# BigBird attention followed by a GELU MLP on one core: dense first batch, one load queue in need order, a hand-set instruction order

## The chip, the cores and the metric

The kernel runs on one core of one Trainium2 chip. The metric is the device time of the core in microseconds (us). Most executions of one kernel agree within 0.5%. One execution of the kernel before fell into a slower state (341.37 us at a mean granted clock of 0.846) and is left out.

Engines are named as in the profile: PE is TensorE's matrix products, PEld its weight loads, DVE is VectorE, ACT is ScalarE, POOL is GpSimd, SP only starts DMAs. All instructions pass through one helper, so the profile gives them all the same source line (L54); groups are told apart by tile names.

## The reference, cut to what matters

```python
# q, k, v: (4 batches, 8 heads, 768 tokens, 64), float32; blocks of 32 tokens, 24 blocks
scores = q @ k.T / sqrt(64)
mask = |block_i - block_j| <= 1  or  block_i in (0, 23)  or  block_j in (0, 23)
mask |= three sampled key blocks for each query block
attn = softmax(where(mask, scores, -1e9))
x = (attn @ v).transpose(0, 2, 1, 3).reshape(3072, 512)
out = gelu(x @ w_in) @ w_out          # w_in (512, 2048), w_out (2048, 512), exact GELU
```

The work goes by half batches of 384 tokens: eight times attention, then a hidden layer (products with `w_in`, then GELU), then output products with `w_out`. They are counted 0 to 7 below; batch 0 is half batches 0 and 1.

## The kernel before

Attention exists in two forms. The *gathered* form (`scores`, `weighted`) computes only the blocks that the mask allows: POOL gathers the sampled key blocks (`gather_k`) and value blocks (`gather_v`) into their own tiles, which needs index arithmetic on DVE and a rotated copy of v in SBUF. The *dense* form (`first_scores`, `first_weighted`) computes all scores and adds the mask as a second product. Before, only the first half of batch 0 is dense.

These are the loads of the opening. The queue of SP takes the first keys and queries, the sampled indices and v; the queue of POOL takes the rest. The weights wait: a one-column memset ordered behind v's casts holds `w_in` back, and `w_out` follows it.

```python
for i, (w, x) in enumerate((("k", k), ("q", q))):
    ...                                           # two heads of k, then of q, as float32
    sp.dma_start(out=first_st[w], in_=x[0, 0:2].rearrange("h (p j) d -> p h (j d)", j=NT))
    if i == 0:
        sp.dma_start(out=raw, in_=...)            # the sampled indices
first_v = load_v(0, sp)                           # six DMAs, each row of 64 values is 256 bytes

def load_v(b, eng, after=None):
    t = stv_pool.tile([P, NT, H, D], F32, tag="st_v", name="st_v")
    ...
    for n in range(NT):
        eng.dma_start(out=t[:, n], in_=v[b, :, n * P:n * P + P].rearrange("h p d -> p h d"))

def after_values():
    for n in range(NT):
        own_v(0, first_v, n, n + 1, dve)          # float32 to bf16
    for c in range(2):
        dve.memset(w_in_sb[:, 0:1, 1024 * c:1024 * c + 1], 0.0)
        load_w_in(c)                              # casting DMA on POOL's queue
```

This is the order of the opening. Each engine runs its instructions in the order in which the program names them, so what stands in `extra` delays what follows on the same engine.

```python
extra = {(0, 3): lambda: first_pair(1), (1, 1): lambda: first_pair(2), (1, 3): lambda: first_pair(3),
         (2, 1): lambda: [after_values(), value_validity()],
         (2, 3): lambda: [first_weighted(0), gather_constants(), key_indices()],
         (3, 1): lambda: [first_weighted(1), load_w_out(0), load_w_out(1)]
         + [f() for f in k_steps(0, 1, range(NPAIR))],
         (3, 3): lambda: [first_weighted(2), rotate_first(), value_columns()]}
for hp in range(NPAIR):
    for t in range(NT):
        first_scores(hp, t)
        extra.get((hp, t), lambda: None)()
first_weighted(NPAIR - 1)
for m in range(MH):
    transpose_x(0, 0, m, st)
value_indices(0, dve)
```

After the opening, rules spread the work. `spread` strews the transposes and gathers for the next half evenly over the eight hidden steps, and `weave` puts a fixed number of output products behind each attention step. A hidden step takes all four 128-row parts of x at once:

```python
def step(m):
    hp_ = sc_pool.tile([P, 2, 512], F32, tag="sc", name="hp")
    for i in range(2):
        for ki in range(KIN):                     # KIN is 4
            pe.matmul(hp_[:, i, 0:HALF], lhsT=w_in_sb[:, ki, (m + i) * P:(m + i + 1) * P],
                             rhs=xT[:, ki, :], start=(ki == 0), stop=(ki == KIN - 1))
    act.activation(g[:, m:m + 2, :], hp_[:, :, 0:HALF], AF.Gelu)
```

The softmax here doesn't subtract the row's maximum and nothing guards it: scores larger than these inputs give would overflow.

## Time and profile before

| | kernel before |
|---|---|
| time, median of 3 runs | 321.12 us (319.97 to 321.38) |
| span of the profiled run, mean granted clock | 320.1 us, 0.973 |
| TensorE busy | 273.6 us, 85% of the span |
| first hidden product / second hidden layer starts | 37.6 us / 81.5 us |

From the page of the profile of before: the span; busy time by engine; busy tenths of PE and the granted clock in 40 slices of 8 us; then, of its list of DMA issues, the load of `w_out`, with its size and the time from issue to landing.

```profile
span 320.1 us, 8104 instructions
PE 273.6 (85%) x3560; PEld 163.4 (51%) x3560; DVE 136.8 (43%) x366; ACT 156.1 (49%) x206; POOL 100.7 (31%) x149
...
PE   1778596698993998989997998989997989899995
PEclk9999899799996899999999999999999999999999
...
w_out_sb<-in_moe_w_out_dram POOLq DMA_DIRECT2D x2, 1024.0 KB, 32.3
```

TensorE is the bottleneck, but the slices show holes in the opening (the first digits) and one near 96 to 104 us (the 3), with the clock reduced behind some of them. `w_out` took 32 us from its issue at 24.8 us.

The view of what each engine waited for names the holes of PE (total us, times, longest):

```profile
PE s L54 <- POOL kg L54: 5.7, 2, 5.1
PE op L54 <- DMA w_out_sb<-in_moe_w_out_dram: 5.1, 2, 3.1
...
PE psx L54 <- DVE x L54: 2.0, 1, 2.0
```

`s <- kg` is a score product that waits for gathered keys; `op <- w_out` an output product that waits for its weights; `psx <- x` the transposition of x that waits for its normalisation.

The timeline of before around the last of these (start, length, engine, operation, in brackets the idle time before it and who ended it):

```profile
34.06 0.85 DVE L54 SCALAR_TENSOR_TENSOR base_v<-colf,slotm,base_v 128x22 f32<-128x22 f32 x3
35.35 0.56 DVE L54 TENSOR_TENSOR x<-og,rc 128x384 bf16<-128x384 f32 x1
35.96 0.45 PE L54 MATMUL psx<-ident,x 128*128 128x128 bf16 x5 [2.00 <-DVE x L54]
37.60 4.42 PE L54 MATMUL hp<-xT,w_in_sb 128*128 128x384 bf16 x16 [0.52 <-DVE xT L54]
```

DVE does index arithmetic (from 31.35 us on, `base_v` is the end of it) for the gathers of the next half first, and only then normalises the last head pair, for which PE has long been waiting.

A view of chosen stretches. I cut the run where a hidden layer's first product starts, and once (51.4 us) where the first hidden layer ends. Columns: stretch, length, busy us of PE, PEld, DVE, ACT, POOL with instruction counts, granted clock, DMA share, GB/s.

```profile
0.00:37.60 37.60, 22.34 (x348) 13.54 (x349) 26.55 (x105) 20.80 (x27) 14.51 (x40) 1.00 0.88 162
...
51.40:81.50 30.10, 23.64 (x354) 14.77 (x354) 11.62 (x30) 13.15 (x18) 8.07 (x7) 0.89 1.12 210
81.50:126.00 44.50, 37.45 (x521) 22.73 (x520) 19.61 (x41) 19.65 (x26) 19.63 (x29) 0.92 0.53 108
...
158.00:196.00 38.00, 34.24 (x476) 21.02 (x475) 16.82 (x39) 19.55 (x26) 19.15 (x22) 1.00 0.58 106
196.00:228.00 32.00, 29.93 (x419) 17.92 (x419) 13.16 (x26) 16.41 (x22) 7.78 (x14) 1.00 0.39 102
```

PE is idle for 15.3 us before 37.6 us, 6.5 us in the stretch of the `w_out` waits, 7.1 us in that of the key wait, and 2 to 4 us in each later one. A few per cent of the matrix product records can be missing from a trace, so small differences of PE's busy time mean nothing.

### The profile page before, as it was taken

What the parts mean: (1) busy time and instruction counts of PE and PEld (TensorE: products, weight loads), DVE (VectorE), ACT (ScalarE), POOL (GpSimd) and SP (SyncE); (2) the same over time, 40 slices, a digit from 0 to 9 for tenths busy, and PEclk for the clock granted to TensorE, in tenths of its full rate; (3) what the DMA queues carried; (4) which work ended last, traced back from release to release, by engine and by line L of the source; (5) the groups of instructions that cost most, each with busy time, mean ns of one, the idle gap of its engine ahead of it and who ended that gap; (6) DMA issues with size and microseconds to landing.
All of it is one profiled execution on the core that took longest, in us unless ns stands there. A gap on an engine that the chain in (4) does not pass through costs nothing. (4 is left out here: it accounts for less than half of the span.)

```text
span 320.1 us, 8104 instructions
## 1 busy us (share of the span) xinstructions
PE 273.6 (85%) x3560; PEld 163.4 (51%) x3560; DVE 136.8 (43%) x366; ACT 156.1 (49%) x206; POOL 100.7 (31%) x149
## 2 busy tenths in 40 slices
PE   1778596698993998989997998989997989899995
PEld 0345353464561654646564654646564645465642
DVE  5488871066460355415632555245440461035001
ACT  3587066254343660466256651576247634753620
POOL 6133422610054554343445554321244430000000
PEclk9999899799996899999999999999999999999999
DMA  6949999999960049007791590009500000010001
GB/s 156 205 94 167 216 234 199 191 209 237 250 132 0 20 76 173 35 0 175 198 202 29 69 199 33 2 2 240 167 2 2 35 35 33 2 35 35 33 35 66
DMA packets 42131, 33.79 MB, mean 106 GB/s; under 512 B 26096, under 2 KB 36464, under 8 KB 42096
## 3 DMA queue, kind: packets, MB, share of 16 engines
q1 hardware_dynamic: 31024, 23.18, 29.3%
q0 software_dynamic: 11072, 10.09, 20.2%
q8 instruction: 28, 0.46, 0.6%
q14 instruction: 7, 0.06, 0.1%
HBM read 27.34 MB, written 6.29 MB: 105 GB/s over the span
## 5 line engine op out<-in xcount | busy, mean ns | idle before, releaser
L54 PE MATMUL op<-w_out_sb,g 128*128 128x512 bf16 x384 | 97.3, 390 | 5.1 <-DMA w_out_sb<-in_moe_w_out_dram 5.1
L54 ACT ACTIVATE g<-hp 128x768 bf16<-128x768 f32 x64 | 51.7, 810 | 85.5 <-PE hp L54 85.5
L54 PE MATMUL hp<-xT,w_in_sb 128*128 128x384 bf16 x512 | 88.4, 331 | 1.9 <-DVE os L54 0.9
L54 PEld LDWEIGHTS <-w_in_sb 128*128 128x128 bf16 x512 | 49.5, 99 | 36.9 <-issue 4.4
L54 ACT ACTIVATE pt<-s 128x1024 bf16<-128x1024 f32 (+2 forms) x84 | 51.6, 687 | 26.1 <-PE s L54 13.3
L54 DVE TENSOR_TENSOR pt<-pt,mask_x 128x768 bf16<-128x768 bf16 x28 | 17.4, 620 | 96.6 <-ACT pt L54 96.4
L54 POOL INDIRECT_COPY v_gat<-v_flat,idx_v 128x1024 f32 (+1 forms) x21 | 33.4, 1592 | 78.4 <-issue 36.6
L54 POOL INDIRECT_COPY kg<-tk,idx_k 128x704 f32 x28 | 34.1, 1219 | 67.8 <-issue 58.1
L54 PEld LDWEIGHTS <-g 128*128 128x128 bf16 x384 | 34.5, 100 | 38.5 <-issue 8.3
L54 DVE COPY tk<-ps 128x768 bf16<-128x768 bf16 x16 | 15.3, 957 | 33.2 <-PE ps L54 33.2
L54 ACT ACT_TABLE_LOAD x16 | 20.5, 1283 | 17.9 <-PE s L54 9.3
L54 DVE COPY os<-op 128x512 f32<-128x512 f32 x24 | 16.6, 692 | 24.2 <-PE op L54 22.2
L54 PEld LDWEIGHTS <-tk 64*128 64x128 bf16 (+1 forms) x312 | 15.1, 98 | 20.2 <-issue 16.7
L54 PE MATMUL ps<-ident,st 128*64 128x128 bf16 x384 | 15.0, 229 | 8.0 <-ACT st L54 7.7
L54 PE MATMUL s<-tq,kg 64*128 64x32 bf16 x616 | 12.3, 174 | 10.8 <-POOL kg L54 5.7
L54 PEld LDWEIGHTS <-pt 128*32 128x32 bf16 (+1 forms) x868 | 19.8, 97 | 2.5 <-DVE x L54 0.3
L54 PE MATMUL s<-tq,tk 64*128 64x128 bf16 (+1 forms) x216 | 18.5, 252 | 1.3 <-ACT pt L54 0.7
L54 PEld LDWEIGHTS <-st 128*64 128x64 bf16 x384 | 12.0, 114 | 13.4 <-ACT st L54 7.9
L54 DVE TENSOR_TENSOR x<-og,rc 128x384 bf16<-128x384 f32 x32 | 17.8, 558 | 1.1
L54 ACT ACTIVATE pd<-sd 128x768 bf16<-128x768 f32 x16 | 13.0, 813 | 9.9 <-PE sd L54 9.9
L54 PEld LDWEIGHTS <-kg 64*128 64x128 bf16 x616 | 11.2, 94 | 12.5 <-issue 6.3
L54 PE MATMUL psx<-ident,x 128*128 128x128 bf16 x96 | 9.3, 219 | 9.0 <-DVE xT L54 3.7
(110 smaller groups left out, 233.2 us busy)
## 6 DMA issues: line engine op xcount, KB each, us to landing
st_v<-in_v_dram SPq DMA_DIRECT2D x24, 256.0 KB, 6.1
out_dram<-os SPq DMA_DIRECT2D x24, 256.0 KB, 3.1
v_flat<-v_flat SPq DMA_DIRECT2D x8, 594.0 KB, 7.3
v_flat<-v_flat SPq DMA_DIRECT2D x8, 396.0 KB, 5.5
st<-in_k_dram POOLq DMA_DIRECT2D x7, 384.0 KB, 7.2
st<-in_q_dram POOLq DMA_DIRECT2D x7, 384.0 KB, 10.3
w_in_sb<-in_moe_w_in_dram POOLq DMA_DIRECT2D x2, 1024.0 KB, 13.1
w_out_sb<-in_moe_w_out_dram POOLq DMA_DIRECT2D x2, 1024.0 KB, 32.3
```

Source lines behind the costliest of these rows:

```text
L54: return self._tc.keep_in_program_order(f(*args, **kwargs))
```

## The change

The intent: batch 0 becomes dense in both halves, so that no gather, value rotation or index arithmetic stands in the way at the start. v is loaded with six neighbouring tokens per partition, as rows of 1,536 bytes instead of 256, and its loads go on POOL's queue between the remaining q/k and the weights, in the order in which they are needed. The rules `weave` and `spread` go; strings of tokens say the order of every step by hand. x is transposed per head pair as soon as it is ready, and a hidden layer begins its first two pairs of products on the first three head pairs of x.

```diff
+OPENING = """
+A0 k1 F00 F01 F02 F03 F04 q1 P0 F05 F10 F11 k2 F12 q2 F13 J0 F14 F15 F20 J1 V00 ... X2 V30 V31 L1 V32 H X3"""
 ... (FIRST, SECOND, SPARSE)
+DENSE = """
+H H G t2 u2 H H H M3 t3 u3 H K03 K02 H H O3 S0 O1 K13 K12 C10 L3 O1 C11 O2 D0 W0 S1 O3 D1 O2 W1 S2 O1 X0
+K11 O1 E0 O2 C12 D2 E1 W2 S3 O1 X1 O1 E2 D3 O1 W3 E3 O2 X2 Y O1 K10 O2 X3 H"""
 ... (SPARSE2, DENSE2, LAST_SPARSE, LAST)
-    sc_pool = ... bufs=2;  og_pool = ... bufs=2;  mm_pool = ... bufs=2
+    sc_pool, og_pool, mm_pool = psum(opening, 0, (3, 1, 1))     # and (2, 2, 2) after the opening
+    act.dma_start(out=raw, in_=...)
-    first_v = load_v(0, sp)
+    first_v = stv_pool.tile([P, H, NT * D], F32, tag="st_v", name="st_v")
 ... (after the last q/k load of batch 0)
+    for i in range(2):
+        pool.dma_start(out=first_v[:, 4 * i:4 * i + 4],
+                       in_=v[0, 4 * i:4 * i + 4].rearrange("h (p j) d -> p h (j d)", j=NT))
+    for c in range(2):
+        load_w_in(c)
-    def first_scores(hp, t):
-        c = slice(t * P, t * P + P)
+    def first_scores(hb, hp, t, masked=False):
+        c = slice(t, S, NT)                       # keys with a step of six
+        cq = slice(hb * HALF, hb * HALF + HALF)
+    def pair_x(hb, hp, og, st):                   # x and its transposition per head pair
+        x = st["x", hb, hp] = x_pool.tile([P, MH, P], BF16, tag="x", name="x", bufs=3)
+        normalise(x.rearrange("p m (h d) -> p m h d", h=2), og, MH)
+        def begin():
+            for m in (0, 2):
+                mms(m, range(KIN - 1))
         def step(m):
-            (all four parts, GELU)
+            mms(m, range(KIN - 1, KIN) if m < 4 else range(KIN))
+            gelu(m)
```

In the strings F and V are dense scores and weighted values, S and W gathered ones, D and E the dense query blocks, X a transposition of x, H a hidden step (the first H of a half is `begin`), O output products, t and u transposes of the next keys and queries, K and C gathers of keys and values, J casts of v, P loads of `w_out`, L loads of a batch's q and k. "K13" gathers keys for half 1, head pair 3.

## The prediction

> I predict **292 us**, against 321.1 before, with 285 to 301 as the range for 8 times in 10.
>
> **What bounds the kernel now.** TensorE: 273.6 us of 320.1 busy (page, busy table), and from 81.5 us on 215 of 238.5 us (windows). The loss is before 81.5 us and in single holes:
> - First exponential at 11.0 us, last at about 33.5; first MLP product at 37.6 us (timeline). TensorE is idle from 34 to 36 us while VectorE does index arithmetic before it normalises the last head pair. Then the clock is 0.50 in 38-40 us (windows). The Trainium skill, "TensorE: Matmul & The Clock Gate", Part 1, says that an idle window of about 3.4 us halves the clock; this trace agrees in kind (0.50 after this hole and those at 52-54, 58-60 and 96-101 us).
> - Two waits for w_out, 2.0 and 3.1 us, at 52 and 58 us (waits, timeline); issued at 24.8 us, the weights landed some 32 us later.
> - A wait of 5.1 us for gathered keys at 96-101 us, then clock 0.50.
> - Per half batch 1.5 to 4 us of small holes: serial x transposes (0.4 to 0.7 us each), exponential table load, xdT.
>
> **What the change does, costed.**
> - Batch 0's second half: gathered attention goes (per head pair 0.81 us scores + 0.65 weighted + about 0.84 for dense query blocks: 9.6 us TensorE with transposes), dense comes (24 x 0.33 + 4 x 1.14 = 12.5 us). TensorE +3 us, ScalarE +6 us (24 exponentials of 0.72 against 4 x (1.84 + 0.81)). Price: 3 us on the path. In return batch 0 needs no gather, value rotation (2.4 MB) or index work.
> - Loads in need order: casting loads run at about 330 GB/s of source (w_in: 4.2 MB in 13 us). Estimate: k, q, v in by 18 us, w_in by 31, w_out by 44, batch 1 by 60: all just in time. The w_out waits and most of the kg wait go.
> - MLP products begun on three quarters of x hide the last normalisation and transposition: about 1 us per half, eight times.
> - Hand-set order, three score buffers in the opening, last output in two pieces (0.3 us).
>
> **Sum.** First exponential at 9.6 us, 24 of them ScalarE-bound at 0.72 us plus hiccups: 30.5. First hidden layer done at 42.5 us (51.4 before). Second dense half with output products: 26.3 us of TensorE work plus 1.5: next boundary at 70 (81.5 before). Then the seven stretches, before 44.5, 32, 38, 32, 37, 30, 25; after 35.5, 31, 35.5, 31, 35, 29, 24 = 221. In all 291-292. Savings: 11 us before the boundary, 9 in the stretch with the kg wait, about 8 spread over the rest.
>
> **Chances:** faster by over 2%: 0.94; within 2%: 0.04; slower: 0.02.
>
> **What would show it.** First MLP product near 31 us at full clock; no w_out wait; no kg wait over 1 us; second hidden layer starting near 70 us; stretches 1 to 3 us shorter; TensorE busy about 265 us.
>
> **What would make it wrong.** The dense scores now load weights with a step of six bf16 elements. The Trainium skill, "SBUF — State Buffer", on cachelines, calls up to eight free; this trace has no strided weights. If such a load takes twice its 0.10 us, 3 to 5 us are lost. VectorE waits in order for v (twice): a late landing stalls TensorE. Batch 1's k and q queue behind w_out and may be late near 55 us. Single og and mm buffers in the opening may serialise it.

## The result, and the profile after

| | before | after |
|---|---|---|
| time, median of 4 runs each, same rounds | 321.25 us (319.97 to 321.48) | 293.02 us (292.19 to 293.86) |
| ratio of after to before, 95% interval | | 0.9126 (0.9091 to 0.9161) |
| span of the profiled run, clock | 320.1 us, 0.973 | 290.4 us, 0.994 |
| TensorE busy | 273.6 us (85%) | 265.4 us (91%) |

A ratio here and below is the mean time of one kernel's runs over that of the kernel before in the same rounds, so it is not quite the ratio of the medians.

The page of after, the same lines:

```profile
span 290.4 us, 7951 instructions
PE 265.4 (91%) x3477; PEld 166.6 (57%) x3516; DVE 132.5 (46%) x352; ACT 163.1 (56%) x215; POOL 95.1 (33%) x134
...
PE   0899799999999989999999999499999999999995
PEclk9999999999999999999999999799999999999999
...
w_out_sb<-in_moe_w_out_dram POOLq DMA_DIRECT2D x2, 1024.0 KB, 26.2
```

The holes of the opening are gone, except for the 7.4 us before the first product, in which the first keys land and are cast. There is one new hole, the 4 in slice 26 (182 to 189 us), with the only reduced clock. `w_out` still takes 26 us to land, but it is now issued at 9.2 us.

What PE waited for in after:

```profile
PE s L54 <- POOL kg_all L54: 3.9, 1, 3.9
PE hp L54 <- ACT g L54: 3.8, 6, 1.3
```

No `w_out` wait is left, and the wait for x is gone. The wait for gathered keys is there again, at another place. The second line is new: the begun hidden products leave both score buffers occupied, so the next ones wait for a GELU.

The stretches of after, cut by the same rule:

```profile
0.00:30.60 30.60, 21.13 (x344) 14.47 (x345) 16.16 (x41) 21.63 (x29) 13.14 (x28) 1.00 1.03 217
...
43.80:70.60 26.80, 26.38 (x333) 15.18 (x335) 15.19 (x41) 20.37 (x26) 1.88 (x9) 1.00 0.61 124
70.60:106.30 35.70, 34.13 (x483) 21.93 (x486) 18.70 (x45) 20.82 (x27) 15.47 (x20) 1.00 0.45 100
...
136.50:168.80 32.30, 31.98 (x468) 20.85 (x473) 15.84 (x39) 19.43 (x26) 14.87 (x19) 1.00 0.35 76
168.80:204.50 35.70, 30.55 (x417) 18.78 (x420) 14.50 (x26) 16.31 (x22) 12.03 (x16) 0.95 0.65 136
```

All stretches side by side. The boundaries of before are 37.6, 51.4, 81.5, 126, 158, 196, 228, 265 and 295.4 us, those of after 30.6, 43.8, 70.6, 106.3, 136.5, 168.8, 204.5, 237 and 267 us:

| stretch | before | after | predicted |
|---|---|---|---|
| opening, to the first hidden product | 37.6 | 30.6 | about 31 |
| first hidden layer | 13.8 | 13.2 | about 12 |
| outputs of half 0, attention of half 1 | 30.1 | 26.8 | 26.3 + 1.5 |
| half 1 (gathered attention of batch 1 begins) | 44.5 | 35.7 | 35.5 |
| half 2 | 32.0 | 30.2 | 31 |
| half 3 | 38.0 | 32.3 | 35.5 |
| half 4 | 32.0 | 35.7 | 31 |
| half 5 | 37.0 | 32.5 | 35 |
| half 6 | 30.4 | 30.0 | 29 |
| half 7, outputs alone from there on | 24.7 | 23.4 | 24 |

A caution on these boundaries: in after the first product of a hidden layer is a begun one, which runs before x is complete. By the first GELU of each layer, the second hidden layer starts at 83.2 us in before and at 75.9 us in after. So 7.3 us of the gain lie before it, not 10.9, and the next layer follows after 32.8 us instead of 44.7, a gain of 11.9 us and not 8.8.

The total hit to 1 us, but not every stretch did. Half 4 became 3.7 us *longer* than before. The chain that ended last in after, followed through its hole, shows how (start, length, what):

```profile
166.56 1.65 POOL v_gat L54
168.21 3.00 POOL st L54 x4
171.21 2.02 issue
173.23 1.64 POOL v_gat L54
...
180.88 3.87 issue
184.75 1.19 POOL kg_all L54
...
185.99 0.91 PE s L54 x25
```

POOL works through its queue: gathers of values, four DMA issues (`st`, 3.0 us in a row), more gathers. The last key gather before the hole ends is the one for head pair 0 (K10, last in the string DENSE), and the very first score product of the next half needs head pair 0. Before a gather POOL shows about 2 us of "issue" (1.3 to 2.5), so gathers that are recorded as 1.19 us start some 3.3 us apart. The 3.87 us before the last gather are longer than that, for a reason that the profile doesn't show. POOL's busy share of 33% hides that it is nearly full here.

### The profile page after: what moved, and what is told of

Same layout as the page of the kernel before. It is cut to its first block, busy times and chain, and to the rows that moved or that the text cites. A ratio compares the mean times of both kernels' runs of the same rounds, so it can differ in the third digit from the quotient of the medians.

```text
span 290.4 us, 7951 instructions
## 1 busy us (share of the span) xinstructions
PE 265.4 (91%) x3477; PEld 166.6 (57%) x3516; DVE 132.5 (46%) x352; ACT 163.1 (56%) x215; POOL 95.1 (33%) x134
## 4 chain that ended last, share of the span: by engine, by line
PE 81%; ACT 5%; issue 5%; POOL 3%; DVE 3%; DMA 2%; ACTq 0%
PE op L54 26%; PE hp L54 25%; PE s L54 12%; PE og L54 9%; PE ps L54 4%; ACT kg_all L54 2%; PE psx L54 2%; DMA raw<-in_sampled_blocks_dram 2%; ACT g L54 2%; POOL v_gat L54 2%; PE od L54 1%; PE sd L54 1%; DVE pt_all L54 1%; POOL st L54 1%; POOL kg_all L54 1%
## 5 line engine op out<-in xcount | busy, mean ns | idle before, releaser
L54 PE MATMUL op<-w_out_sb,g 128*128 128x512 bf16 (+1 forms) x361 | 90.3, 373 | 2.3 <-issue 0.6
L54 ACT ACTIVATE pt_all<-s 128x1024 bf16<-128x1024 f32 (+2 forms) x72 | 44.2, 686 | 30.8 <-PE s L54 30.0
L54 POOL INDIRECT_COPY kg_all<-tk,idx_k 128x704 f32 x24 | 30.2, 1258 | 56.0 <-issue 51.5
L54 DVE TENSOR_TENSOR pt_all<-pt_all,mask_x 128x768 bf16<-128x768 bf16 x24 | 16.0, 667 | 60.1 <-ACT pt_all L54 60.1
L54 PEld LDWEIGHTS <-pt_all 128*32 128x32 bf16 (+2 forms) x840 | 23.9, 101 | 6.8 <-issue 1.5
L54 DVE COPY os<-op 128x512 f32<-128x512 f32 (+1 forms) x25 | 16.6, 666 | 23.1 <-PE op L54 23.1
L54 PEld LDWEIGHTS <-st 128*64 128x64 bf16 x384 | 12.8, 116 | 15.7 <-issue 7.5
L54 ACT ACTIVATE v_gat<-s 128x768 bf16<-128x768 f32 x24 | 18.3, 811 | 5.9 <-PE s L54 5.7
L54 ACT ACTIVATE kg_all<-s 128x768 bf16<-128x768 f32 x24 | 17.6, 819 | 2.8 <-PE s L54 2.7
L54 DVE COPY tq<-ps 128x768 bf16<-128x768 bf16 (+1 forms) x16 | 14.9, 928 | 6.6 <-PE ps L54 4.9
L54 PEld LDWEIGHTS <-kg_all 64*128 64x128 bf16 (+1 forms) x672 | 14.2, 94 | 5.7 <-POOL kg_all L54 4.1
```

Of the source, the lines that this page charges most:

```text
L54: return self._tc.keep_in_program_order(f(*args, **kwargs))
```

## The experiments

Twelve kernels were run. In the first call the kernel before took 321.12 us, in the second 321.47, in the third 321.76 (medians). Every kernel gave correct results. Kernels made from after are compared with after over their ratios to before (after itself was 0.9126). Most ratios have an interval of about 0.003 to 0.005 on either side, so a difference between two of them isn't resolved under about 1.5 us (two a_ kernels) to 2.3 us (two b_ kernels). Six kernels (b_) are the kernel before with one or two parts of the change, or with one step moved; six (a_) are after with one part undone or altered.

| kernel | what | median us | ratio to before |
|---|---|---|---|
| b_idx | before, index arithmetic later | 320.96 | 0.999 |
| b_weights | before, weights loaded early | 333.88 | 1.0388 |
| b_dense | before, batch 0 dense | 317.26 | 0.9879 |
| b_dense_w | both of these | 338.57 | 1.0523 |
| b_oneq | b_weights, v on the same queue ahead of the weights | 316.69 | 0.9848 |
| b_dense_oneq | b_dense and b_oneq | 317.57 | 0.988 |
| a_nobegin | after, no begun products | 294.78 | 0.9167 |
| a_gate | after, weights held back until v is in | 295.34 | 0.9183 |
| a_vnat | after, v in 256-byte rows, same queue | 296.25 | 0.9221 |
| a_v6sp | after, v in 1,536-byte rows, on SP's queue | 294.03 | 0.9145 |
| a_vnatsp | after, v in 256-byte rows, on SP's queue | 318.02 | 0.988 |
| a_swapk | after, key gathers in the order of need | 287.23 | 0.8932 |

The theory after the result was: the gain before 81.5 us comes from the weights arriving in time, from dense work in place of index work, and from better order; a gain per half comes from the begun products. The rivals: one of these alone does it, the rest being carried along.

### b_idx: the hole at 34 to 36 us, closed alone

```diff
-             (3, 3): lambda: [first_weighted(2), rotate_first(), value_columns()]}
+             (3, 3): lambda: [first_weighted(2), rotate_first()]}
 ...
     for m in range(MH):
         transpose_x(0, 0, m, st)
+    value_columns()
     value_indices(0, dve)
```

> The kernel before, with the index work (value_columns) moved behind the x transposes. My theory: in the kernel before the first MLP product is held by VectorE's index arithmetic, so it starts near 36 us instead of 37.6, but the second half then still waits for w_out, whose landing (about 54 and 61 us) does not move; total within 0.5 us of before, and the hole at 52-54 us grows by what was won. Rival: the start of the MLP is itself on the critical path; then the total falls by 1.6 to 3 us.

Measured: 320.96 us, ratio 0.999 (0.9939 to 1.0041). PE's wait for x fell from 2.00 to 0.71 us, the half clock at 38 to 40 us was gone (1.00 in that window), and GELU started at 40.0 instead of 41.7 us. But the two waits for `w_out` grew to 3.25 and 2.87 us (6.1 in all, 5.1 before), and the second hidden layer's GELU started at 82.7 instead of 83.2 us. So a visible hole of 2 us and its half clock were worth next to nothing: what ended last in that part was the landing of `w_out`, which did not move.

### b_weights: weights early, v left alone

```diff
     for w in "kq":
         st["st", w, 1] = load_qk(0, w, 1)
+    for c in range(2):
+        load_w_in(c)
 ... (the two memsets and load_w_in behind v's casts removed)
     first_pair(0)
+    load_w_out(0)
+    load_w_out(1)
```

> The kernel before, with w_in and w_out issued at once behind q and k, not held until v has landed. My theory: both w_out waits (5.1 us) and the half clock after them go; the stretch from 51.4 to 81.5 us falls from 30 to 24-27 us; total 5 to 8 us less, unless v now lands so late (it shares the engines) that the opening grows by 1 to 3 us. Rival: the opening moves the same bytes whatever their order, so the wait only moves to v or to the gathered keys, and the total changes by less than 2 us.

Measured: 333.88 us, ratio 1.0388 (1.034 to 1.0436): 12.8 us slower, the opposite of what I had expected. The first hidden product came at 58.9 instead of 37.6 us. The `w_out` waits were gone, but the view of what DVE waited for has a new line for b_weights:

```profile
DVE v_flat L54 <- DMA st_v<-in_v_dram: 19.4, 3, 7.6
```

v, alone on SP's queue, no longer kept up with the weights on POOL's queue. The gate that I had read as the fault of before was protecting v. I had allowed 1 to 3 us for a later v, not this; the experiments on v below follow from it.

### b_dense: batch 0 dense, nothing else

The second half of batch 0 takes `first_scores` and `first_weighted` with its own queries, the masks are built for all 24 blocks, its gathers and the value rotation go, and the key tiles become one tile to make room. The order of its steps is mine, one output piece behind each score tile, not tuned.

```diff
+        if b == 0:
+            steps = []
+            for hp in range(NPAIR):
+                for t in range(NT):
+                    steps.append((lambda hp=hp, t=t: first_scores(hp, t, 1), int(hp + t > 0)))
+                    if t == 1 and hp:
+                        steps.append((lambda hp=hp: first_weighted(hp - 1, 1), 0))
+            return steps + [(lambda: first_weighted(3, 1), 1), (X_(0), 0), (X_(1), 0), (X_(2), 0)]
```

> The kernel before, with batch 0's second half dense too (no gathers, no value rotation for batch 0), loads and order left alone. My theory: the dense half alone is worth little: 3 us more TensorE work against an earlier w_out (2.4 MB of rotation less in front of it); total 2 to 6 us less. Rival: the dense half is the main source of the 28 us; then 10 us or more less.

Measured: 317.26 us, ratio 0.9879 (0.9827 to 0.9931). No `w_out` wait is left, although `w_out` is still issued late; the 2.4 MB of value rotation that went at the same time are gone, which may be why. The clock was 0.999, and the large key wait became four of 1.33, 1.26, 0.59 and 0.60 us. The dense half took 31.9 us (47.3 to 79.2) with PE busy for 28.2. The 26.8 us of after are no measure for it, because that stretch ends at a begun product: from the first GELU of the first hidden layer to that of the second it is 42.4 us here (38.3 to 80.7) and 42.0 us in after (33.9 to 75.9). So the dense form, with the traffic that it saves, is worth 4 us; what the hand-set order adds in this half is not shown.

### b_dense_w: dense, and weights early

Edit: the two above together.

> Both of the last two edits on the kernel before. My theory: the effects need each other: 10 to 14 us less than before (w_out waits gone, rotation gone, first MLP product still near 37 us because index work and pools are as before). Rival (independent effects): just the sum of the two single edits.

Measured: 338.57 us, ratio 1.0523 (1.0442 to 1.0605). DVE waited 20.9 us for v, and the first hidden product came at 59.1 us. Dense work doesn't cure it; the starved v is the same.

### a_nobegin: after without the begun products

```diff
         def begin():
-            for m in (0, 2):
-                mms(m, range(KIN - 1))
+            pass
         def step(m):
-            mms(m, range(KIN - 1, KIN) if m < 4 else range(KIN))
+            mms(m, range(KIN))
             gelu(m)
```

> The changed kernel without the MLP products begun on three quarters of x (each hidden layer starts when x is whole). My prediction said about 1 us per half, eight times, so 6 to 8 us more. Rival: the trace of the changed kernel shows TensorE waiting 3.8 us in six pieces for the first GELUs just after these products, so part of what is hidden is given back: 2 to 5 us more. No change would mean that the holes are filled by other work anyway.

Measured: 294.78 us, ratio 0.9167 (0.9138 to 0.9195): 1.3 us slower than after, a little under what is resolved, against the 8 us of my prediction. What PE waited for in a_nobegin:

```profile
PE psx L54 <- DVE x L54: 3.5, 3, 1.8
...
PE hp L54 <- ACT g L54: 0.9, 1, 0.9
```

Without `begin`, PE waits 3.5 us for x, but the wait for GELU falls from 3.8 to 0.9 us. Begun products trade one wait for another: they hide x, and then stand in two buffers that only GELU frees.

### a_gate: after with the weights held back until v is in

```diff
+    def weights_in():
+        for c in range(2):
+            dve.memset(w_in_sb[:, 0:1, 1024 * c:1024 * c + 1], 0.0)
+            load_w_in(c)
 ... (in OPENING: "P0" and "P1" removed from their places, "N P0 P1" set behind J2)
```

> The changed kernel with the weight loads held back until v has been used for the third head pair (about 23 us, as in the kernel before). My theory: the first MLP product stays near 31 us (first half of w_in lands by then), w_out lands near 43 and 49 us, one wait of 1 to 4 us for it returns, and batch 1's keys are late too: 3 to 7 us more. Rival: load order is without effect once batch 0 is dense: within 1 us.

Measured: 295.34 us, ratio 0.9183 (0.9149 to 0.9218): 1.8 us slower than after, less than the 3 to 7 us expected. The first hidden product waited 0.88 us for `w_in`, and an output product 1.33 us for `w_out` at 48.6 us. So with everything else in place, loading the weights early is worth about 2 us, hardly more than is resolved. v lands so early on its new way that even weights held back behind it are nearly in time.

### a_vnat: after with v in rows of 256 bytes

```diff
-    first_v = stv_pool.tile([P, H, NT * D], F32, tag="st_v", name="st_v")
+    first_v = stv_pool.tile([P, NT, H, D], F32, tag="st_v", name="st_v")
 ...
-    for i in range(2):
-        pool.dma_start(out=first_v[:, 4 * i:4 * i + 4], ...)
+    for n in range(NT):
+        pool.dma_start(out=first_v[:, n], in_=v[0, :, n * P:n * P + P].rearrange("h p d -> p h d"))
 ...
-        c = slice(t, S, NT)
+        c = slice(t * P, t * P + P)
```

> The changed kernel with v loaded in the old layout (256-byte packets, neighbouring tokens on neighbouring partitions) and score weights read without a step. v landed at about 16.2 us and its first use is at 17.6, so 1.4 us of slack. My theory: v lands 3 to 5 us later, the opening and the weights behind it slip: 1 to 3 us more, first MLP product at 32 to 33 us; weight loads of the scores fall from 0.12-0.15 to 0.10 us without effect. Rival: the stepped weights cost more than the packets save: less time than the changed kernel.

Measured: 296.25 us, ratio 0.9221 (0.9186 to 0.9255): 3.0 us slower than after. PE waited 2.04 us for v at 21.1 us, and the first hidden product came at 33.1 instead of 30.6 us. It also took away the step of six in the key weights; whatever that gave was less than what the later v cost.

### a_swapk: after with the key gathers in the order of need

```diff
 DENSE (and DENSE2 the same):
-... O3 S0 O1 K13 K12 C10 L3 O1 C11 ... X0 K11 O1 E0 ... Y O1 K10 O2 X3 H
+... O3 S0 O1 K10 K11 C10 L3 O1 C11 ... X0 K12 O1 E0 ... Y O1 K13 O2 X3 H
```

> The changed kernel with the key gathers of the second half batch in the order of their use (head pair 0 first instead of last) in the two stretches that gather it last. The trace shows TensorE waiting 3.9 us at 182-186 us for just this gather, and a clock of 0.7 after it. My theory: order alone is at fault, the wait goes: 3.5 to 5.5 us less, 287.5 to 289.5 us. Rival: GpSimd is full in that stretch (each gather blocks it for about 3.3 us), so the wait moves to the next gather: less than 1.5 us.

Measured: 287.23 us (286.57 to 288.3), ratio 0.8932 (0.8901 to 0.8963): about 6 us faster than after, the fastest kernel of all. Its PE waits have no `s <- kg_all` line any more:

```profile
PE ps L54 <- ACT st L54: 7.5, 1, 7.5
PE hp L54 <- ACT g L54: 3.8, 6, 1.3
```

The stretch of half 4, cut by the same rule in a_swapk:

```profile
170.30:200.50 30.20, 29.16 (x419) 18.36 (x423) 13.91 (x26) 16.31 (x22) 12.13 (x16) 1.00 0.78 158
```

It fell from 35.7 to 30.2 us and the clock is 1.00: 3.9 us of waiting and the slow clock behind it. By starts of GELU the other stretches differ from those of after by at most 0.3 us, but for the opening, which took 1.4 us longer in this run. Gathers in the order of need remove the hole, with the same number of gathers.

But the order alone does not make it. In after, half 6 follows the same order of gathers (DENSE2), without the four DMA issues (L3) between them, and it has no hole:

```profile
247.07 1.19 POOL L54 INDIRECT_COPY kg_all<-tk,idx_k 128x704 f32 x1 [2.07 <-issue]
...
249.83 0.43 PE L54 MATMUL s<-tq,kg_all 64*128 64x32 bf16 x22
```

There the last gather ends 11.3 us after the half began (at 237.0 us), in half 4 it ends 17.1 us after (168.8 to 185.9). So it took both: the gather for head pair 0 placed last, and what the loads of the next batch cost POOL ahead of it (3.0 us of DMA issues; whether the long idle time before the last gather belongs to them is open). Moving the loads instead was not tried.

### b_oneq: before with one queue in need order, v still in rows of 256 bytes

```diff
-    first_v = load_v(0, sp)
 ... (after the last q/k load)
+    first_v = load_v(0, pool)
+    for c in range(2):
+        load_w_in(c)
 ... (the rest as in b_weights)
```

> The kernel before with early weights as in the run that lost 12.8 us, but v issued on the same queue as the weights, ahead of them. In that run v, in 256-byte packets on a queue of its own, was starved by the weights and landed near 25 to 43 us. My theory: the queue decides; in one queue v is served first and lands by 20 to 24 us, w_in by 36, w_out by 50; both w_out waits go and the total is 3 to 7 us less than before. Rival: early weights crowd v out whatever the queue; then still 5 us or more above before.

Measured: 316.69 us, ratio 0.9848 (0.9801 to 0.9895), against 1.0388 for the same early weights with v on its own queue: 17 us lie in the queue that v is on. v landed 9.7 us after issue (median of six loads), the `w_out` waits are gone, and the second hidden layer's GELU starts at 77.9 instead of 83.2 us. The hole at 34 us stayed and grew (2.95 us, then clock 0.50 from 38 to 42 us), and so did the key wait (5.55 us at 96.3 us), as nothing was done about the index work and the gathers.

### b_dense_oneq: this, and batch 0 dense

Edit: b_dense and b_oneq together.

> The same with batch 0's second half dense. Dense alone won 3.9 us. If the two effects add: 7 to 11 us less than before. If one queue only mends what dense already mended (b_dense had no w_out wait left): 3 to 6 us less, about as b_dense. If they need each other: 12 us or more less.

Measured: 317.57 us, ratio 0.988 (0.9829 to 0.993): no better than either alone. Both remove the `w_out` waits, and they can be removed only once. It stands some 24 us above after, though it has the dense batch and the load order. By starts of GELU the difference between the two is spread: 4.8 us up to the first hidden layer, 1.5 up to the second, 8.4 in the next half, then 1.9, 4.2, -3.5 (after's new hole), 5.1, 2.2 and 0.5.

### a_v6sp and a_vnatsp: the rows and the queue of v

```diff
 a_v6sp:
-        pool.dma_start(out=first_v[:, 4 * i:4 * i + 4], ...)
+        sp.dma_start(out=first_v[:, 4 * i:4 * i + 4], ...)
 a_vnatsp: as a_vnat, but
+        sp.dma_start(out=first_v[:, n], in_=v[0, :, n * P:n * P + P].rearrange("h p d -> p h d"))
```

> The changed kernel with v (new layout, 1536-byte packets) on a queue of its own. If packet size sets a queue's share, v gets a fair share and lands about as early: within 2 us of the changed kernel. If a queue of its own is the harm, v lands late: 5 us or more above.

> The changed kernel with v in the old layout (256-byte packets) on a queue of its own. In one queue the old layout cost 3.2 us. My theory: beside 1536- to 4096-byte packets of another queue it is starved, lands at 30 us or later and TensorE waits for it: 8 to 20 us above the changed kernel. Rival: the changed kernel's opening has enough slack: 3 to 5 us, as in one queue.

Measured: a_v6sp 294.03 us, ratio 0.9145 (0.9102 to 0.9188), within 1 us of after. a_vnatsp 318.02 us, ratio 0.988 (0.9831 to 0.993), some 24 us slower than after and 21 us slower than a_vnat. PE in a_vnatsp, what it waited for:

```profile
PE og L54 <- DVE v_flat L54: 23.4, 1, 23.4
```

The DMA view of a_vnatsp from 20 to 32 us: packets and MB of each queue (q1 is SP's, with v alone on it, q0 is POOL's with the weights):

```profile
q0 software_dynamic: 1394, 2.04, 93.3%
q1 hardware_dynamic: 1395, 0.35, 22.4%
```

And of a_v6sp from 8 to 12 us (q0 still moves queries and keys there):

```profile
q1 hardware_dynamic: 507, 0.76, 59.7%
q0 software_dynamic: 499, 0.36, 58.1%
```

In both, the two queues move nearly the same *number* of packets, whatever their size. (Not in every window: from 10 to 12 us a_vnatsp moved 430 packets on q0 and 278 on q1.) With packets of 256 bytes v gets 0.35 of 2.39 MB; with packets of 1,536 bytes it gets 0.76 of 1.12 MB. The Trainium skill, "DMA: Bandwidth & Descriptors", section "Queues, rings and completion order", says that each engine goes round-robin between the queues it has work for, a packet at a time; these counts agree in kind. The page's packet is typically some 9 to 17 descriptors, while the profile counts rows of 256 bytes one by one, so which unit takes turns is not settled here. b_weights shows the same from 20 to 32 us: 1,420 packets of v against 1,415 of the other queue, 0.36 against 2.03 MB; so does b_dense_w (1,426 each). SP's queue is not slow in itself: in before, without the weights beside it, it moved 936 packets of v from 14 to 16 us, in a_vnatsp 328. So small packets on a queue of their own, against large packets on another, got a small share. On one queue (a_vnat, b_oneq) v simply goes first.

The medians of the four combinations:

| v of batch 0, weights early | on POOL's queue, ahead of the weights | on SP's queue, beside them |
|---|---|---|
| rows of 1,536 bytes | after, 293.02 us | a_v6sp, 294.03 us |
| rows of 256 bytes | a_vnat, 296.25 us | a_vnatsp, 318.02 us |

Each of the two parts is worth 1 to 3 us alone, and each protects from the same loss of more than 20 us.

## Why the prediction was right, point by point, and where it was not

- **Total.** 292 us was predicted (285 to 301), 293.02 measured. PE's busy time was predicted as 265 us and came out as 265.4, though the prediction shows no working for that number. That the sum is within about 1 us is partly luck: half 4 was 4.7 us longer than predicted, halves 3 and 5 together 5.7 us shorter.
- **Opening.** Predicted "near 31 us at full clock": 30.6 us, clock 1.00. (The clock of the view does not cover the start: a pair of score products took 0.52 us up to about 11.6 us and 0.32 to 0.37 us from then on.) The start was wrong (first exponential 9.6 predicted, 10.85 measured: the first keys landed 5.8 us after issue instead of 3.1; the indices now come on another queue beside them, which I take for the reason but did not test), but the exponentials then ran with fewer hiccups. Two errors of about 1 us cancel.
- **First hidden layer.** 13.2 us instead of about 12: 1.27 us is a wait for GELU behind the begun products; of this, 0.94 us is there without them too (a_nobegin).
- **`w_out` waits.** They went, as predicted. But a_gate shows that early weights alone are worth 1.8 us (at most a few) in the finished kernel. The prediction read the load order as a matter of *when*; the runs show that it is as much a matter of *beside what*. That 24 us hang on the rows and the queue of v was not in it at all; it was right only because the change does both things well.
- **Second boundary.** Predicted 70, measured 70.6 us. The stretch after it: 35.5 predicted, 35.7 measured. But this boundary is a begun product: by the first GELU, 7.3 us were saved before it, not the 11 predicted, and 11.9 us in the stretch with the kg wait, not 9.
- **"No kg wait over 1 us".** Wrong. The step that failed is "The w_out waits and most of the kg wait go", put into half 4 as "31": a wait of 3.9 us came up there, and 35.7 us was measured. I took the wait of before for a matter of late index arithmetic and load traffic, and did not lay POOL's queue of gathers and DMA issues out in time against the order of need. a_swapk shows the cause: gathers in the order of need remove it, about 6 us with the half clock. Half 6, which has the same order and no hole, shows that the order alone was not enough: the loads of the next batch, which only half 4 has ahead of its last gather, belong to the cause.
- **Begun products.** The mis-sized term is "about 1 us per half, eight times". a_nobegin measures 1.3 us in all. The mechanism is there (3.5 us of waiting for x come back without it), but most is returned as 3.8 us of waiting for GELU (0.9 us without them).
- **Halves 3 and 5.** Predicted 35.5 and 35, measured 32.3 and 32.5. In before PE was idle there for 3.8 and 3.0 us, in after for 0.3 each. So the hand-set order gave more than I had counted, and this hid the error in half 4 and in the begun products.
- **What could go wrong.** Key weights with a step of six did not take twice the time: 123 ns against 96 in a_vnat for keys, 136 against 98 for the mask's block columns (means of the 96 loads of each in the dense scores, up to 71 us). The Trainium skill, "SBUF — State Buffer", section "Door 1: The DMA port swizzle", on cachelines, gives eight bf16 elements as how far one can stride for free; this shows a small cost, not none. a_vnat, which has no such step for the keys and the mask, was no faster, though for another reason. A late v did not stall VectorE here, but a_vnatsp shows that this worry was the right one (23.4 us).
- **The clock.** The Trainium skill, "TensorE: Matmul & The Clock Gate", Part 1, gives about 3.4 us of idle window for half clock. This agrees with the 3.9 us hole of after: the clock is 0.50 in the window from 186 to 188 us behind it. In before the hole was shorter, 2.0 us at 34 to 36 us, and half clock followed all the same; from 34.0 to 37.6 us PE was busy for only about 0.8 us, so it need not be wholly idle. In b_idx the hole was 0.71 us and the clock stayed 1.00.

What stays open: of the gain of 28 us, about 4 go to the dense batch and the load order together (b_dense_oneq), the rows of 1,536 bytes for v give about 3 (a_vnat), and the begun products about 1; these need not add up. The other 20 us or so come with what remains: the hand-set order, the other division of the PSUM buffers in the opening, x transposed per head pair, and its placing. Which of these gives how much wasn't taken apart. The spread over nearly every stretch and the idle time of PE in halves 3 and 5 (3.8 and 3.0 us before, 0.3 after) fit the order as the main part, but that is argued, not shown.

## What to carry to other kernels

Before you read a late load as "issue it earlier", look at which queue it shares the DMA engines with and in what packet size: here small rows on a queue of their own lost to large ones beside them (0.35 against 2.04 MB), and a gate that looks like waste may be what protects them. When an order is set by hand, list for each engine's queue what is needed first and check it against what is placed first, also for an engine that looks two thirds idle. A closed hole is worth something only if nothing else ends at the same time.

## What the Trainium skill lacked or had wrong

- "DMA: Bandwidth & Descriptors", section "Queues, rings and completion order", states the round-robin by packets, but not what follows for mixed sizes. Here 1,395 packets of v against 1,394 of weights in the same 12 us meant 0.35 against 2.04 MB, and 24 us of the kernel's time (a_vnatsp against after).
- "Trainium Kernel Development and Optimization", Key Constraints, says that issuing from several engines only saves the sequencer's issue time. Here the same 256-byte loads on SP's queue instead of POOL's cost 21 us (318.02 against 296.25), so the choice of queue also sets the share and the order.
- "SBUF — State Buffer", on cachelines, lets eight bf16 elements pass as free. Weight loads with a step of six took 123 ns against 96 (keys) and 136 against 98 (mask); small, but not free.
- "TensorE: Matmul & The Clock Gate", Part 1, speaks of an idle window of about 3.4 us. A hole of 2.0 us in a stretch of 3.6 us with about 0.8 us of work was followed by a clock of 0.50. What Part 1 says on frequent short idle times gives no length for them.
- No page has the pace of an indirect copy on GpSimd. One of 704 float32 elements on 128 partitions is recorded as 1.19 us, but about 2 us in which the engine shows nothing go before a gather, also behind a copy (2.19 us) or DMA issues (2.02 us). So two in a row start some 3.3 us apart (219.63 and 222.92 us in after), and POOL's busy share reads too low.
